# Decoding weights with the sign taken by GpSimd, an earlier Exp table load, and new instruction orders

## The chip, the cores and the metric

The kernel runs on one core of one Trainium2 chip. The metric is the time of one execution in microseconds (us), lower is better. The core's engines are called PE (TensorE), DVE (VectorE), ACT (ScalarE), POOL (GpSimd) and SP (SyncE, which here only issues DMAs). Each engine executes its own instructions strictly in order and waits on semaphores for what other engines produce. PEld is the weight-load side of PE.

## The reference, cut to what matters

```python
def _attn_ref(q, k, v, f):                      # B, H, S, D = 8, 8, 576, 64
    scores = np.matmul(q, k.transpose(0, 1, 3, 2)) / np.sqrt(D)
    cum = np.cumsum(np.log(np.clip(f, 0.0001, 1.0)), axis=-1)
    scores = scores + cum[:, :, :, None] - cum[:, :, None, :]   # causal, upper part -1e9
    attn = np.exp(scores - scores.max(-1)); attn /= attn.sum(-1) + 1e-9
    return np.matmul(attn, v)

def _moe_ref(x, w_tok1, w_tok2, w_ch1, w_ch2):  # x: (8, 576, 512) = attention, heads side by side
    h = np.maximum(x^T @ w_tok1, 0) @ w_tok2    # mixes tokens: 576 -> 256 -> 576
    u = x + h^T
    return u + np.maximum(u @ w_ch1, 0) @ w_ch2 # mixes channels: 512 -> 1536 -> 512
```

The four weight matrices of the mixers are float64 in memory. The chip has no float64 arithmetic, so the kernel turns each weight into float32 itself ("decodes" it) from its two 32-bit words, and keeps a rounded high part and a low part for the matmuls.

## The kernel before, in words

**Two stages.** The attention stage covers about the first 392 us. It runs over 32 head pairs (called n0 to n31 here): scores on PE (`score`, L747, with a decay term `fall`, L774, for the six head pairs listed in ND, n0 among them, or a mask, L753), a combined add and row minimum on DVE (`rmin`, L788), Exp with its row sum on ACT (`expo`, L792), transposes on PE (L862) and their copies by ACT and DVE (L872, L870), the product with v on PE (L891). After every second pair, a half of a batch goes through the token mixer (L1245). The second stage is the channel mixer (`chunk`, L1047 to L1049 and L1128 to L1130). It covers the rest; its first products are woven into the last few microseconds of the attention stage.

**Weight decoding** runs beside the attention stage: nine pieces of the token weights early (five of 128x256, four of 128x288), then 24 units of the channel weights of 128x512 each. `decode` (L553) makes one piece in six operations before it is split:

- s1, ACT (L572): the float64's high word, read as a float32, times 2^-112, into `g`. This sets the exponent's range and keeps the sign.
- s2, DVE (L576): shift `g` left by three bits. This aligns exponent and mantissa and pushes the sign out.
- s3, DVE (L580): the exponent bits of `g` into `e`.
- s4, DVE (L584): the low word times that power of two, into `e`.
- s5, POOL (L588): `g` plus `e`.
- s6, DVE (L592): the sign bit of the high word, joined to `g` with a bitwise or.

Then POOL makes the high part (L492) and the low part (L495), and for a channel unit four sums of blocks (L631) and their two parts. `d_g`, the tile with `g` and `e`, has two buffers.

**Order of work.** `ORDER` holds, for every engine, the numbers of its operations in the sequence in which it executes them. A planner (`Plan.run`) only assigns buffers to that sequence. A number n:k stands for k operations from n on. SP's loads are paced in addition: the total of what lies behind a load in flight is kept near 1.2 MB.

**Start.** `decay` (L508) loads f, takes its logarithm on ACT (L526; the small operation of L524 before it brings in the logarithm's table), sums it up on DVE (L528), scales it by -8 on ACT (L536, a Copy) and writes it to DRAM (`decd`, L538), from which later head pairs read it. The first Exp instruction (L792) brings in the Exp table. `fill` (L545) makes 36 small matmuls whose result nobody reads; each needs a free PSUM bank, and the scores of one head pair take all eight banks.

Of the kernel before, what the change touches and what calls it, by code (L numbers as in the profile page):

```python
# [67 lines left out]
    ),  # L68
    DVE=(
# [369 lines left out]
def build(nc, env, dims):  # L439
# [30 lines left out]
    def d_dve(n, fast=False):  # L470
        return 70 + (0.52 if fast else 1.042) * n
# [37 lines left out]
    def decay():  # L509
# [3 lines left out]
        def row(i):  # L513
            return at(w)[:, i, :]
# [38 lines left out]
    def decode(loads, w, hi, lo, tok):  # L553
# [20 lines left out]
        def s2():  # L574
            low, high, g, e = tl()
            nc.vector.tensor_scalar(g, g, 3, None, op0=ALU.logical_shift_left)  # L576
# [960 lines left out]
```

## Time and profile before

| what | us |
|---|---|
| median of 3 runs | 925.55 (924.63 to 926.01) |
| the profiled execution | 927.18 |
| its span, first to last instruction | 925.4 |
| PE busy | 905.5 (98%) |
| PEld busy | 781.3 (84%) |
| DVE busy | 710.2 (77%) |
| ACT busy | 520.6 (56%) |
| POOL busy | 237.2 (26%) |

Shares are of the whole span, which joins stages with different limits. PE's busy time counts a matmul from its start to a modelled end, so a short wait between two matmuls can vanish in it; the weight loads of PEld have no such tail. POOL has nothing to do after the attention stage.

### The profile page before, as it was taken

Reading aid. Unit: us, or ns where it says so; the run is one execution under the profiler, and the core shown is the slowest. Engines: PE = TensorE matmul, PEld = TensorE weight load, DVE = VectorE, ACT = ScalarE, POOL = GpSimd, SP = SyncE. Lnnn points to the kernel's source line nnn. Section 1 sums busy time; section 2 is a strip of 40 time slices with the busy share of each in tenths; the row PEclk is TensorE's granted clock in tenths of the full one; section 3 lists DMA queues with packets and bytes.
Section 4 is the critical chain, followed back from the end, with each engine's and each line's share of the span. In section 5 each row is a group of like instructions: output and inputs, shape, how many; then the busy total and the mean of one; then the engine's idle time right before and its main releaser. Section 6 shows DMA issues by size and latency. Waiting matters only on the chain.

```text
span 925.4 us, 26760 instructions
## 1 busy us (share of the span) xinstructions
PE 905.5 (98%) x10270; PEld 781.3 (84%) x10270; DVE 710.2 (77%) x1894; ACT 520.6 (56%) x1340; POOL 237.2 (26%) x320
## 2 busy tenths in 40 slices
PE   7999999999998999999999999999999999999998
PEld 5688888788887787888888888888888899999998
DVE  7998988888777777754699646986389955995497
ACT  5989998998788988731354123541135412542142
POOL 4577776766665562110000000000000000000000
PEclk9999999999999999999999999999999999999999
DMA  7999999998999698558887878888888799889986
GB/s 237 273 268 281 312 280 292 302 282 274 276 304 285 207 271 224 167 176 293 263 257 234 265 208 245 250 252 261 261 244 247 239 294 303 286 273 298 294 286 220
DMA packets 143871, 242.49 MB, mean 262 GB/s; under 512 B 15936, under 2 KB 71488, under 8 KB 143744
## 3 DMA queue, kind: packets, MB, share of 16 engines
q1 hardware_dynamic: 143648, 240.64, 84.8%
q8 instruction: 81, 1.33, 0.6%
q14 instruction: 46, 0.38, 0.1%
q10 hardware_dynamic: 96, 0.15, 0.0%
HBM read 199.52 MB, written 41.21 MB: 260 GB/s over the span
## 4 chain that ended last, share of the span: by engine, by line
PE 59%; DVE 2%; DMA 2%; POOL 1%; issue 0%; ACT 0%; SPq 0%; DVEq 0%; POOLq 0%
PE bank L1047 9%; PE bank L1049 9%; PE bank L1048 9%; PE bank L1128 9%; PE bank L1130 9%; PE bank L1129 9%; PE bank L1245 2%; DMA d_raw<-ud 1%; DVE pr L788 1%; PE bank L891 1%; PE bank L862 0%; DMA wq<-wd 0%; DMA recd<-rs 0%; POOL sg L495 0%; PE bank L747 0%
## 5 line engine op out<-in xcount | busy, mean ns | idle before, releaser
L792 ACT ACTIVATE pr<-pr,nmin 64x64 f32<-64x64 f32 (+4 forms) x320 | 176.7, 560 | 16.6 <-DVE nmin L788 16.2
L489 ACT ACTIVATE st<-H 128x512 fp32r<-128x512 f32 (+1 forms) x210 | 119.6, 586 | 89.0 <-PE bank L1129 63.3
L1128 PE MATMUL bank<-st,wq 128*128 128x512 f32 (+1 forms) x420 | 154.2, 367 | 0.3 <-DMA wq<-wd 0.3
L1130 PE MATMUL bank<-st,wq 128*128 128x512 f32 (+1 forms) x420 | 154.3, 367 | 0.0
L1129 PE MATMUL bank<-st,wq 128*128 128x512 f32 (+1 forms) x420 | 154.2, 367 | 0.0
L788 DVE CUSTOM_DVE_ANT_0 pr<-bank,cb 128x448 f32<-128x448 f32 (+3 forms) x260 | 108.7, 454 | 6.0 <-PE bank L747 1.8
L747 PE MATMUL bank<-raw 64*64 64x448 f32 (+6 forms) x1408 | 109.5, 397 | 2.6 <-DMA raw<-in_qk 1.3
L498 DVE TENSOR_TENSOR st<-H,st 128x512 fp32r<-128x512 f32 (+1 forms) x150 | 92.4, 631 | 14.6 <-ACT st L489 14.2
L891 PE MATMUL bank<-pf,vr 64*64 64x256 f32 (+3 forms) x2048 | 98.7, 317 | 1.5 <-ACT pf L872 0.5
L983 DVE TENSOR_TENSOR tmp<-bank,tmp 128x512 f32<-128x512 f32 (+1 forms) x80 | 50.2, 632 | 55.6 <-PE bank L1049 42.4
L872 ACT ACTIVATE pf<-bank 128x512 f32<-128x512 f32 x152 | 84.4, 596 | 11.2 <-PE bank L862 5.7
L1128 PEld LDWEIGHTS bank<-st,wq 128*128 128x128 f32 x420 | 78.8, 188 | 10.2 <-issue 0.6
L1130 PEld LDWEIGHTS bank<-st,wq 128*128 128x128 f32 x420 | 78.8, 188 | 9.9
L1129 PEld LDWEIGHTS bank<-st,wq 128*128 128x128 f32 x420 | 78.8, 188 | 9.6
L891 PEld LDWEIGHTS bank<-pf,vr 64*64 64x64 f32 x2048 | 76.4, 134 | 10.0 <-issue 2.0
L747 PEld LDWEIGHTS bank<-raw 64*64 64x64 f32 x1408 | 52.0, 132 | 27.7 <-issue 10.2
L1073 ACT ACTIVATE H<-bank 128x512 f32<-128x512 f32 (+1 forms) x30 | 16.5, 554 | 103.2 <-PE bank L1049 103.1
L1059 ACT ACTIVATE tmp<-bank 128x512 f32<-128x512 f32 (+1 forms) x30 | 16.6, 552 | 101.1 <-PE bank L1049 101.1
L862 PE MATMUL bank<-ident,pr 64*128 64x64 f32 x1536 | 65.0, 225 | 5.4 <-issue 2.1
L862 PEld LDWEIGHTS bank<-ident,pr 64*128 64x128 f32 x1536 | 58.8, 139 | 11.2 <-issue 5.0
L922 POOL TENSOR_TENSOR xt<-xt,rb 128x64 f32<-128x64 f32 (+1 forms) x64 | 52.5, 840 | 49.7 <-DVE xt L910 19.6
L792 ACT ACTIVATION_READ_ACCUMULATOR pr<-pr,nmin 128x1 f32 (+1 forms) x320 | 63.2, 198 | 0.0
(171 smaller groups left out, 2109.9 us busy)
## 6 DMA issues: line engine op xcount, KB each, us to landing
wq<-wd SPq DMA_DIRECT2D x420, 256.0 KB
raw<-in_qk SPq DMA_DIRECT2D x32, 576.0 KB
cb<-decd SPq DMA_DIRECT2D x26, 576.0 KB
d_raw<-in_w_ch SPq DMA_DIRECT2D x48, 256.0 KB
wd<-sg SPq DMA_DIRECT2D x24, 512.0 KB
vr<-in_v SPq DMA_DIRECT2D x64, 160.0 KB
rb<-recd SPq DMA_DIRECT2D x32, 320.0 KB
wd<-sg SPq DMA_DIRECT2D x24, 384.0 KB
```

What stands on the lines that cost most here:

```text
L489: nc.scalar.activation(out, in_, func, scale=scale)
L498: nc.vector.tensor_tensor(out, in_, asf(hi), op=ALU.subtract)
L747: nc.tensor.matmul(at(buf)[HALF[h], of : of + n], q[:, i0 : i0 + D], k[:, j0 : j0 + n], start=t not in (0, 1), stop=not nd, skip_group_che ...
L788: nc.vector.tensor_tensor_reduce(o, x, y, -1.0 / D**0.5, c0[:m, NS + z : NS + z + 1] if t == 5 else 3e38, op0=ALU.add, op1=ALU.min, accum_ ...
L792: nc.scalar.activation(x, x, AF.Exp, bias=E["nmin"][sm][:m, t : t + 1], scale=-1.0, accum_out=E["rec"][rm][:m, c : c + 1])
L862: nc.tensor.transpose(at(ps[s])[:, k * D : (k + 1) * D], at(pr)[r, x, :, :].rearrange("p a b -> p (a b)"), E["ident"][r, r])
L872: p.op("ACT", d_act(512), lambda src_=src_, o=o: nc.scalar.activation(o(), src_(), AF.Copy), rd=[ps[s]], wr=[(pt, s)], bufs=[ps[s], pt])
L891: nc.tensor.matmul(at(av[z])[o, 256 - w : 256], at(vr)[r, vblk(j), :], at(pt)[r, c : c + w], start=j == 4, stop=gi == 2, skip_group_check= ...
L1047: nc.tensor.matmul(o, wt[:, 0, :], h_, start=(first and k == 0), stop=False, skip_group_check=True)
L1128: nc.tensor.matmul(o, wt[:, 0, :], h_, start=(first and x == 0), stop=False, skip_group_check=True)
L1129: nc.tensor.matmul(o, wt[:, 1, :], h_, start=False, stop=False, skip_group_check=True)
L1130: nc.tensor.matmul(o, wt[:, 0, :], l_, start=False, stop=(x == FX - 1), skip_group_check=True)
```

## The change

The sign is no longer taken from the high word at the end. GpSimd multiplies the scaled `g` by 0.0, which leaves a zero that has the sign of `g`, in `e`. VectorE then shifts `g` and joins that sign in one instruction (the new s6, which stands where s2 stood). s3, s4 and s5 follow as before; what was the last operation of a decode is gone. Per decode DVE has three instructions instead of four and POOL two instead of one. DVE has 33 operations less in all, POOL 33 more.

In `decay`, an Exp of the one-column tile `lnx` stands just before the Copy of L536, so the Exp table is brought in there.

`ORDER` is new for all five engines in the attention stage. Most operations move by some places (PE by at most 15, SP and ACT by at most 22); the channel mixer's part is kept. The core of the diff, with the head of each order:

```diff
 PE:
-14:12 145 135 146 136 26:2 139 155 28:3 156 140 185 31:11 193 202 42:3 188 45:4 165 49 168 171 ...
+14 145 135 139 15:3 136 146 140 18 155:2 19:20 193 185 202 188 39:10 165 168 171 ...
 DVE:
-6 8:3 53:3 62 153 63 57 64 137:2 147 149 71 66 72 143 151 73 161 159 157 141 163 80:2 ...
+6 8:3 54:3 63 138 64 143 65 149 153 137 147 151 72 157 73:2 161 159 141 163 81:3 ...
 ACT:
-3:3 7 11 52 61 70 154 150 144 152 79 162 142 160 158 148 164 88 197 195 ...
+4 3 5 7 11 52 61 70 150 154 148 152 158 79 164 142 144 160 201 162 88 195 ...
 POOL:
-0 56 58:2 65 67:2 74 76 83 77 85:2 92 94 101 95 103:2 110 ...
+0 53 62 57:3 66 71 67:2 75 80 84 76 85 77 86 89 98 93:2 102 95 103:2 107 116 111 ...
 SP:
-2 1 132 51 50 60 181 69 12:2 133:2 78 184 87 182 ...
+2 1 132 51 50 60 69 133 181 12:2 182 134 78 184 87 ...
 decay:
+        def neg():
+            nc.scalar.activation(E["lnx"], E["lnx"], AF.Exp)
+            return nc.scalar.activation(row(0), row(1), AF.Copy, scale=-8.0)
-        p.op("ACT", d_act(S, False), lambda: nc.scalar.activation(row(0), row(1), AF.Copy, scale=-8.0), rd=["c"], wr=["f"], bufs=[w])
+        p.op("ACT", d_act(S, False), neg, rd=["c"], wr=["f"], bufs=[w])
 decode:
         def s2():
             low, high, g, e = tl()
-            nc.vector.tensor_scalar(g, g, 3, None, op0=ALU.logical_shift_left)
+            nc.gpsimd.tensor_scalar(asf(e), asf(g), 0.0, None, op0=ALU.mult)
+
+        def s6():
+            low, high, g, e = tl()
+            nc.vector.scalar_tensor_tensor(g, g, 3, e, op0=ALU.logical_shift_left, op1=ALU.bitwise_or)
-        def s6():
-            low, high, g, e = tl()
-            nc.vector.scalar_tensor_tensor(g, high, 0x80000000, g, op0=ALU.bitwise_and, op1=ALU.bitwise_or)
-        p.op("DVE", d_dve(w, True) , s2, wr=[gb], bufs=[gb], port=True)
+        p.op("POOL", d_pts(w), s2, port=True, rd=[gb], wr=[(gb, 1)], bufs=[gb])
+        p.op("DVE", d_dve(w), s6, port=True, rd=[(gb, 1)], wr=[gb], bufs=[gb])
         p.op("DVE", d_dve(w, True) , s3, rd=[gb], wr=[(gb, 1)], bufs=[gb], port=True)
         p.op("DVE", d_dve(w) , s4, port=True, rd=rd, wr=[(gb, 1)], bufs=[rb, gb])
         p.op("POOL", d_ptt(w), s5, port=True, rd=[(gb, 1)], wr=[gb], bufs=[gb])
-        p.op("DVE", d_dve(w), s6, port=True, rd=rd, wr=[gb], bufs=[rb, gb])
```

In these numbers 14 to 49 are the fills; 145, 135, 139 and 155 the four score groups of n0 and 146, 136, 140, 156 their decay terms; 185, 193, 202 and 188 the scores of n1; 165, 168, 171 the transposes of n0. On SP 132 and 181 load q and k of n0 and n1, 133 and 134 v of n0, 182 a half of v of n1, 50 to 78 token weights, 12 and 13 write `decd`, 184 reads it for n1. On DVE 137 to 163 (odd, and 138) are the row minima of n0; 53 to 55 and 57 belonged to the first decode before, 54 to 56 do now (54 is the join).

## Rows read from the trace of the kernel before

**Rows 1.** Windows: us; PE, PEld, DVE, ACT, POOL busy (instructions); clock; DMA; GB/s.
```profile
9.43:57.00 47.57, 43.22 (x834) 32.14 (x832) 47.19 (x187) 40.69 (x121) 28.51 (x40) 1.00 0.90 259
57.00:120.00 63.00, 62.66 (x1310) 52.83 (x1304) 56.58 (x214) 57.83 (x179) 47.43 (x63) 1.00 0.95 295
120.00:250.00 130.00, 127.87 (x2629) 108.51 (x2630) 111.18 (x399) 114.49 (x336) 90.42 (x116) 1.00 0.93 285
250.00:345.00 95.00, 90.80 (x1878) 77.87 (x1871) 73.18 (x276) 80.64 (x240) 57.07 (x77) 0.98 0.89 266
345.00:392.00 47.00, 45.01 (x934) 39.01 (x929) 36.35 (x122) 38.35 (x111) 7.48 (x9) 1.00 0.73 203
392.00:925.00 533.00, 529.66 (x2678) 467.16 (x2669) 381.42 (x686) 185.30 (x350) 3.43 (x4) 1.00 0.83 258
```

**Rows 2.** Windows of the start, same columns.
```profile
8.00:13.80 5.80, 5.23 (x70) 3.09 (x73) 4.30 (x16) 1.33 (x4) 2.54 (x4) 1.00 0.74 228
13.80:25.00 11.20, 9.34 (x158) 6.32 (x158) 11.08 (x52) 11.19 (x34) 5.94 (x10) 1.00 0.89 272
```

**Rows 3.** Windows, line L576 alone: DVE busy (instructions).
```profile
9.43:57.00 47.57, 3.47 (x11) 1.00 0.90 259
57.00:345.00 288.00, 11.50 (x22) 0.99 0.92 281
```

**Rows 4.** Groups by line and shape, DVE, 9 to 60 us: busy us, mean ns.
```profile
L592 DVE SCALAR_TENSOR_TENSOR d_g<-d_raw,d_g 128x256 uint32<-128x256 uint32 x5 | 2.1, 415 | 0.0
...
L592 DVE SCALAR_TENSOR_TENSOR d_g<-d_raw,d_g 128x288 uint32<-128x288 uint32 x4 | 1.8, 448 | 0.0
```

**Rows 5.** Groups by line and shape, POOL, whole span.
```profile
L492 POOL TENSOR_SCALAR sg<-d_g 128x512 fp32r<-128x512 f32 x48 | 30.5, 640 | 10.2 <-DVE d_g L592 7.6 <-DMA wd<-sg 1.7
...
L492 POOL TENSOR_SCALAR t1h<-d_g 128x256 fp32r<-128x256 f32 x5 | 2.2, 447 | 4.8 <-DVE d_g L592 4.8
L492 POOL TENSOR_SCALAR t2h<-d_g 128x288 fp32r<-128x288 f32 x4 | 2.0, 501 | 2.6 <-DVE d_g L592 2.6
```

**Rows 6.** Timeline of the start: start us, us, what [idle before, releaser].
```profile
2.96 0.20 ACT L524 ACTIVATE lnx<-rec 128x1 f32<-128x1 f32 x1
...
4.43 0.68 ACT L526 ACTIVATE xt<-xt 128x576 f32<-128x576 f32 x1 [1.27 <-DVE xt L525]
...
6.61 0.68 ACT L536 ACTIVATE xt<-xt 128x576 f32<-128x576 f32 x1 [1.49 <-DVE xt L528]
...
8.57 0.79 SPq L538 DMA_DIRECT2D decd<-xt  x2
...
9.43 0.29 DVE L576 TENSOR_SCALAR d_g<-d_g 128x256 uint32<-128x256 uint32 x1 [1.51 <-ACT d_g L572]
...
13.71 1.28 ACT L792 ACT_TABLE_LOAD   x1
...
15.00 0.35 ACT L792 ACTIVATE pr<-pr,nmin 64x64 f32<-64x64 f32 x1
```

**Rows 7.** Waits: us in total, times, longest; POOL in 9 to 57 us.
```profile
POOL d_g L588 <- DVE d_g L584: 13.2, 5, 6.8
```

**Rows 8.** Waits of the whole span.
```profile
DVE d_g L592 <- POOL d_g L588: 2.3, 3, 1.0
```

**Rows 9.** Timeline of PE at the start.
```profile
4.22 2.50 PE L545 MATMUL bank<-ident 128*64 128x48 f32 x22
...
8.00 1.85 PE L747 MATMUL bank<-raw 64*64 64x448 f32 x20 [1.28 <-DMA raw<-in_qk]
...
14.64 1.67 PE L545 MATMUL bank<-ident 128*64 128x48 f32 x22
```

**Rows 10.** Line L545: duration ns min/median/max, first and last start.
```profile
L545 PE MATMUL bank<-ident x72: 222/222/343, 1.8 to 22.2; 128*64 128x48 f32 x72
```

**Rows 11.** Timeline around 289 us.
```profile
289.29 0.89 PE L862 MATMUL bank<-ident,pr 64*128 64x64 f32 x19 [2.12 <-issue]
```

**Rows 12.** Window behind it, columns as in rows 1.
```profile
289.80:293.20 3.40, 3.40 (x66) 3.23 (x64) 1.50 (x3) 3.40 (x10) 3.40 (x4) 0.50 0.76 246
```

399 rows, old and new, of tables (ACT, DVE, PE, POOL) are left out of this document.

## The prediction

> **What bounds the kernel now.** I read the page's busy shares first, then windows cut where the limits change, then the groups by line, the waits, and the timeline of the first 25 us. The windows decide it [rows 1]. From 392 us on PE is busy 529.66 of 533.00 us; no instruction there is changed, so those 533 us stay. The attention stage has two parts. From 9.43 to 57 us DVE is busy 47.19 of 47.57 us, while PEld is busy 32.14 (68%). After 57 us PEld has 83 to 84% in every stretch, and PE is idle only 0.34 + 2.13 + 4.20 + 1.99 = 8.66 us up to 392 us. So DVE sets the pace up to 57 us: it leaves 0.38 us unused in 47 us, and PE, at 43.22 us busy, starves in between (its matmul tails hide part of that, the weight loads do not). From 57 us on PE is close to its own limit, with DVE at 241 of 288 us up to 345 us [rows 1]: DVE time saved there mostly becomes idle time.
>
> The front of the stage is therefore where the change can pay. Microseconds that DVE loses or gains before 57 us move all that comes behind, because behind it PE has a full queue.
>
> **The change part by part.** The sum is made against the profiled execution, 927.18 us (span 925.4, and 1.8 around it); the median of the runs is 925.55, 1.63 below it. I carry the difference over to the median.
>
> *Shift gone from DVE.* One DVE instruction per decode, s2, goes. In the DVE-bound stretch that is 11 instructions with 3.47 us [rows 3]. The new join takes the place of s6; both read two SBUF operands in one pass, so I take 415 ns at 128x256 and 448 ns at 128x288 for both [rows 4]: no difference. The trace shows no such join; below, it could cost no less than the shift alone, 3.47/11 = 0.315 us, which would add 11 x 0.1 = 1.1 us of gain, and I put the same 1.1 us above. Term: -3.47.
>
> *Sign on POOL.* 33 more POOL instructions, each like L492's one-input pass: 447, 501 and 640 ns [rows 5]. Between 9.43 and 57 us that is 5 x 0.447 + 4 x 0.501 + 2 x 0.64 = 5.5 us on an engine that is busy 28.51 of 47.57 us [rows 1], so it fits. But the first join now stands behind it: DVE's first decode instruction starts at 9.43 us right behind ACT [rows 6], and now starts one POOL pass later. That is 0.447 us and hand-overs, say 0.55; between 0.45 and 0.9 (the second sign stands directly behind the first). DVE has nothing else to do then, so this is lost. Later joins stand further behind their signs in the order. At the other end of a decode the way gets shorter: the hand-over from s5 to DVE and back to POOL is gone. Term: +0.55.
>
> *What queues behind a waiting join.* DVE executes in order, so behind a join that waits stand row minima, and behind those ACT's Exp and PE's transposes. POOL in turn often stands still on s5, waiting for s4: 13.2 us in 5 waits in the same stretch [rows 7], and a sign behind such an s5 waits with it. Before, DVE waited for POOL in s6, 2.3 us in 3 of 33 cases [rows 8]. I take nothing beyond that; the upper end is rival A.
>
> *Exp table.* ACT loads it from 13.71 for 1.28 us, right in front of the first Exp at 15.00 [rows 6]. The new Exp stands behind L526, which ends at 4.43 + 0.68 = 5.11; the Copy behind it waits 1.49 us for DVE's scan, until 6.61. Load and one-column instruction take 1.28 + 0.20 = 1.48 us and fill that gap to 0.02 us, so the Copy and the two writes of `decd` at 8.57 do not move. If the cover were gone it would cost 1.28 us on that branch, which has 8.57 - 7.29 = 1.28 us of slack. What is gained: between 13.80 and 25 us ACT is busy 11.19 and DVE 11.08 of 11.20 us [rows 2], both full. Taking 1.28 us from ACT alone leaves DVE as the limit, so it adds nothing to DVE's term but lets it come through. Between 0 and -1.28, I take 0.
>
> Of the same step the Trainium skill ("ScalarE: Activation LUTs", section What ACT_TABLE_LOAD costs) says that a switch costs a load of about 1283 ns and a drain of about 1380 ns. The row agrees with the load (1.28) and not with the drain: the first Exp starts 0.01 us behind the load. With the drain the Copy would come about 1.4 us later and the `decd` writes at most 0.2 us later, so the sum would stay.
>
> *Fills and first scores.* Before, 12 fills stood ahead of the first scores, and PE worked through most of them from 4.22 to 6.72 us. The new order keeps one; PE then waits for q and k until 8.00 us [rows 9]. The first 22 fill matmuls take 2.50/22 = 0.114 us each, 22 later ones 1.67/22 = 0.076, and single ones last 343 ns at most against 222 in the median [rows 9, 10]. So PE ran at the lower of its two clock levels at first and had reached the higher one when scores began. The window's clock column shows 1.00 there, which the pace contradicts. Now the first scores begin after about 4 us of idling, likely at the lower level. At half the clock the 5.23 us of work in 8.00 to 13.80 us [rows 2] lasts up to 5.2 us longer. DVE has the joins, s3 and s4 of two decodes to do meanwhile, some 2.5 us at 0.42 each. Between 0 and 5.2 I take 1.0, nearer the low end, since the new order then runs all scores and 20 fills without a gap. Term: +1.0.
>
> The Trainium skill ("TensorE: Matmul & The Clock Gate", section What's actually happening) has the same behaviour as a rule: the array starts throttled and sustained activity releases it. The trace agrees by the fills' pace, 0.114 against 0.076 us.
>
> *57 to 345 us.* DVE loses 22 shifts, 11.50 us [rows 3], POOL gains 22 x 0.64 = 14.1 us on 195 of 288 us [rows 1, 5]. PE is idle 0.34 + 2.13 + 4.20 = 6.67 us there. From -6.7 (all of it) to +2 (POOL's queue delays the products that release the token mixer); I take about an eighth of PE's idle time: -0.9.
>
> *New orders elsewhere.* q and k of n1 are issued behind two other loads (a 262 kB weight piece and a v half); the PE operation that needs them stands behind 20 fills now. Taken as 0, between -1 and +1.
>
> Sum: -3.47 + 0.55 + 1.0 - 0.9 = -2.8 us. The profiled execution would be 924.4, the median 922.7.
>
> **The rivals.**
>
> *A: joins wait for POOL and the gain is eaten.* For: POOL's 13.2 us of standing on s5 [rows 7], in order, with signs behind; against: POOL has 19 us free before 57 us. At 0.25 us per join, 11 joins take 2.8 us: 925.5.
>
> *B: slower, PE starts at the low clock and stays there.* Place: PE, 8 to about 20 us. If low until the first transposes at 20 us, the 5.2 us above come in full and some 2 us more from the scores of n1 and the fills in front of them (a fifth of the 9.34 us of PE work in 13.80 to 25 us [rows 2], where PE has free time to make up the rest). I count 7 us against gains of 3.8 without the 1.0: +3.2, 928.7. It decides from 3.8 + 1.85 = 5.65 us of delay on. For: 11 fills are moved from idle time to behind scores; each needs a bank that DVE has to free. Against: scores, decay terms and fills stand close together there.
>
> *C: more comes through.* PE stood still for 2.12 us with nothing that the profile shows, and the granted clock was then 0.50 for 3.40 us [rows 11, 12]. That is 2.12 + 1.70 = 3.8 us that need not recur with another order. With it: 918.9. The same time results if half of PE's idle time after 57 us goes. Against: such a pause may come at another place.
>
> *D: it does not do what it says.* The early Exp brings no table, or the first real Exp loads it again. That leaves 1.28 us on ACT at 13.7 us: 924.
>
> **How the numbers follow.** Forecast 0.40 (920.5 to 924), A with D 0.25, B 0.20, C 0.15. What a measurement here can tell from no change is about 0.2%, 1.85 us: faster is below 923.7. Faster: C and nine tenths of the forecast and a little of D, 0.53. Within: the rest of the forecast, most of A, 0.25. Slower: B and some of A's worse end, 0.22. The range from 917.5 to 928.5 takes in C with its 1.1 us for a cheaper join, and B almost to its price.
>
> **What would show it.** Right: DVE's first decode instruction starts near 10.0 us; a table load at 5.1 us and none at 13.7; the scores of n4 and what follows begin 2 to 4 us earlier than before, at an unchanged distance from there to the end; three DVE instructions per decode. Wrong: idle time of DVE ahead of the joins with POOL as releaser, over 3 us before 57 us (A); the granted clock or the score matmuls at half pace beyond 13 us (B); the lead at 57 us lost or doubled by 392 us.

## The result

The changed kernel takes 932.62 us (median of 4 runs, 931.96 to 934.91) against 925.09 us before: a ratio of 1.0085 (95% interval 1.0065 to 1.0104), 7.5 us slower. The forecast was 922.7 us, and faster.

The page of the changed kernel opens with the engines' busy time:

```profile
PE 906.9 (97%) x10270; PEld 781.3 (84%) x10270; DVE 705.8 (76%) x1861; ACT 521.6 (56%) x1341; POOL 279.0 (30%) x353
```

DVE has 33 instructions less, POOL 33 more, as meant. But POOL's busy time grew from 237.2 to 279.0 us, by 41.8 us: 1.27 us for each new instruction, where the forecast had 0.45 to 0.64. The groups of POOL by line and shape name it (L579 is the new sign):

```profile
L579 POOL TENSOR_SCALAR d_g<-d_g 128x512 f32<-128x512 f32 x24 | 36.0, 1501 | 14.2 <-ACT d_g L575 14.2
L491 POOL TENSOR_SCALAR sg<-d_g 128x512 fp32r<-128x512 f32 x48 | 31.2, 651 | 1.4 <-DMA wd<-sg 1.0
...
L579 POOL TENSOR_SCALAR d_g<-d_g 128x256 f32<-128x256 f32 x5 | 4.2, 849 | 5.8 <-ACT d_g L575 5.8
...
L579 POOL TENSOR_SCALAR d_g<-d_g 128x288 f32<-128x288 f32 x4 | 3.7, 930 | 1.1 <-ACT d_g L575 1.1
```

The sign takes 849, 930 and 1501 ns; L491 (the former L492 of [rows 5]) still takes 651 ns for the same 512 columns. The waits of the whole span show who pays (us in total, times, longest):

```profile
DVE d_g L583 <- POOL d_g L579: 18.1, 15, 3.6
```

L583 is the new join. DVE stands still for POOL 18.1 us, where it did so for 2.3 us before [rows 8], and behind the join stand the row minima that ACT and PE need. The windows, with the stretches and columns of [rows 1]:

```profile
9.43:57.00 47.57, 42.21 (x818) 32.54 (x812) 44.53 (x173) 38.63 (x120) 37.61 (x51) 1.00 0.83 251
57.00:120.00 63.00, 60.57 (x1280) 50.75 (x1281) 55.32 (x196) 54.37 (x160) 53.90 (x64) 1.00 0.92 283
120.00:250.00 130.00, 126.56 (x2556) 106.66 (x2549) 105.58 (x383) 113.13 (x342) 103.08 (x127) 1.00 0.92 278
```

Up to 57 us DVE is no longer full (44.53 of 47.57 us against 47.19). Between 57 and 250 us PE is idle for 5.9 us where it was idle for 2.5, and gets 3836 matmuls done instead of 3939. The lateness shows in one row per kernel, that of the weight loads of the scores, whose last number is the start of the last one. First the kernel before, then the changed one:

```profile
L747 PEld LDWEIGHTS bank<-raw x1408: 129/133/135, 8.0 to 372.6; 64*64 64x64 f32 x176
```

```profile
L750 PEld LDWEIGHTS bank<-raw x1408: 128/133/228, 7.4 to 378.6; 64*64 64x64 f32 x176
```

The last score starts 6.0 us later; from there to the end it is 552.5 us (931.1 - 378.6) against 552.8 (925.4 - 372.6). So the loss arose in the attention stage, and the channel mixer neither adds nor gives back anything.

The start of ACT in the changed kernel (timeline, as [rows 6]) shows the early Exp where it should be:

```profile
4.73 0.68 ACT L529 ACTIVATE xt<-xt 128x576 f32<-128x576 f32 x1 [1.59 <-DVE xt L528]
5.43 1.28 ACT L519 ACT_TABLE_LOAD   x1
6.73 0.20 ACT L519 ACTIVATE lnx<-lnx 128x1 f32<-128x1 f32 x1
6.91 0.68 ACT L520 ACTIVATE xt<-xt 128x576 f32<-128x576 f32 x1
...
14.95 0.67 ACT L795 ACTIVATE pr<-pr,nmin 128x448 f32<-128x448 f32 x1 [0.85 <-DVE nmin L791]
```

The load is hidden, no second one stands ahead of the first real Exp, and yet that Exp starts at 14.95 us (15.00 before): it waits for a row minimum. PE's start (timeline, as [rows 9]) shows why, in part:

```profile
7.39 3.90 PE L750 MATMUL bank<-raw 64*64 64x448 f32 x28 [3.12 <-DMA raw<-in_qk]
```

28 score matmuls take 3.90 us, 0.139 each, where 20 took 1.85, 0.093 each [rows 9]: PE starts at a lower pace, as one of the steps had it, though the granted clock of the window from 8.00 to 13.80 us reads 1.00 in both profiles. (Widths are mixed in both rows; a run below has the same 28.)

### The profile page after: what moved, and what is told of

The parts are those of the page before. It is cut to its first block, busy times and chain, and to the rows that moved or that the text cites. A ratio compares the mean times of both kernels' runs of the same rounds, so it can differ in the third digit from the quotient of the medians.

```text
span 931.1 us, 26767 instructions
## 1 busy us (share of the span) xinstructions
PE 906.9 (97%) x10270; PEld 781.3 (84%) x10270; DVE 705.8 (76%) x1861; ACT 521.6 (56%) x1341; POOL 279.0 (30%) x353
## 4 chain that ended last, share of the span: by engine, by line
PE 76%; DMA 8%; DVE 6%; POOL 5%; ACT 2%; issue 2%; SPq 1%; DVEq 0%; ACTq 0%; POOLq 0%
PE bank L1050 9%; PE bank L1051 9%; PE bank L1052 9%; PE bank L1131 9%; PE bank L1132 9%; PE bank L1133 9%; PE bank L1248 7%; PE bank L750 5%; PE bank L894 4%; PE bank L865 3%; DVE pr L791 2%; DMA cb<-decd 2%; POOL d_g L579 1%; DMA raw<-in_qk 1%; DMA wd<-sg 1%
## 5 line engine op out<-in xcount | busy, mean ns | idle before, releaser
L795 ACT ACTIVATE pr<-pr,nmin 128x320 f32<-128x320 f32 (+4 forms) x320 | 176.8, 557 | 14.1 <-DVE nmin L791 13.3
L750 PE MATMUL bank<-raw 64*64 64x448 f32 (+6 forms) x1408 | 114.0, 403 | 6.5 <-DMA raw<-in_qk 3.1
L894 PE MATMUL bank<-pf,vr 64*64 64x128 f32 (+3 forms) x2048 | 97.9, 315 | 0.7 <-ACT pf L875 0.3
L750 PEld LDWEIGHTS bank<-raw 64*64 64x64 f32 x1408 | 55.3, 134 | 35.4 <-issue 11.5
L865 PEld LDWEIGHTS bank<-ident,pr 64*128 64x128 f32 x1536 | 59.4, 139 | 11.1 <-ACT pr L795 2.6
L494 POOL TENSOR_TENSOR sg<-d_g,sg 128x512 fp32r<-128x512 f32 x48 | 62.1, 1298 | 1.0
```

The source lines that it names most:

```text
L750: nc.tensor.matmul(at(buf)[HALF[h], of : of + n], q[:, i0 : i0 + D], k[:, j0 : j0 + n], start=t not in (0, 1), stop=not nd, skip_group_che ...
L795: nc.scalar.activation(x, x, AF.Exp, bias=E["nmin"][sm][:m, t : t + 1], scale=-1.0, accum_out=E["rec"][rm][:m, c : c + 1])
L865: nc.tensor.transpose(at(ps[s])[:, k * D : (k + 1) * D], at(pr)[r, x, :, :].rearrange("p a b -> p (a b)"), E["ident"][r, r])
L894: nc.tensor.matmul(at(av[z])[o, 256 - w : 256], at(vr)[r, vblk(j), :], at(pt)[r, c : c + w], start=j == 4, stop=gi == 2, skip_group_check= ...
```

## The experiments

Times are medians; each ratio is against the kernel before in runs on the same chip. That kernel's median was 925.04 us beside the first four runs, 925.42 beside the next four and 926.26 beside the last three, so small differences between runs of different groups are read from ratios.

**The sign as a two-step instruction.**

```diff
-nc.gpsimd.tensor_scalar(asf(e), asf(g), 0.0, None, op0=ALU.mult)
+nc.gpsimd.tensor_scalar(asf(e), asf(g), 0.0, -0.0, op0=ALU.mult, op1=ALU.add)
```

> The changed kernel with the sign made by a two-step instruction on GpSimd (times 0.0, plus -0.0, which keeps the sign) in place of the one-step multiply. Theory S (the price of the sign): the one-step form costs 1.50 us at 128x512 where the two-step L492 costs 0.64; POOL becomes late and the joins wait. Then the sign falls to about 0.64 us, POOL's busy time from 279 to 255 us, the joins' waits from 18 us to under 8, and the time from 932.6 to 926 to 928 us. Theory O (the new orders are worse by themselves): the sign gets cheaper but the time stays over 930.5. Theory C (cold start alone): the 2.1 us that n2 is late stay, and with them nearly all of the loss; over 930.5.

Measured: 922.11 us, ratio 0.9967 (0.9950 to 0.9983). A second step in this one instruction is worth 10.5 us. POOL's busy time is 253.1 us, 25.9 less. The sign's group in POOL, and the join's wait:

```profile
L579 POOL TENSOR_SCALAR d_g<-d_g 128x512 f32<-128x512 f32 x24 | 15.3, 639 | 18.6 <-ACT d_g L575 18.6
```

```profile
DVE d_g L583 <- POOL d_g L579: 7.0, 6, 2.3
```

The join waits 11.1 us less. The last score starts at 368.2 us, 10.4 us earlier than in the changed kernel:

```profile
L750 PEld LDWEIGHTS bank<-raw x1408: 129/133/227, 7.3 to 368.2; 64*64 64x64 f32 x176
```

Theory S holds, and by more than it said: the whole loss was the price of the sign, and with the price that the forecast had used the kernel is faster than before. Theories O and C fall as causes of the loss.

**Which two-step form.**

```diff
-nc.gpsimd.tensor_scalar(asf(e), asf(g), 0.0, None, op0=ALU.mult)
+nc.gpsimd.tensor_scalar(asf(e), asf(g), 0.0, 1.0, op0=ALU.mult, op1=ALU.mult)
```

> The changed kernel with the sign as a two-step instruction of two multiplies (times 0.0, times 1.0). Theory F1 (a form with its second step left out is the slow one, any two-step form is quick): the sign costs about 0.64 us at 128x512 and the time is 921 to 924, as with times and plus. Theory F2 (only the pair times and plus is quick): the sign costs 1.5 us or more and the time is 931 to 934.

Measured: 922.07 us, ratio 0.9969 (0.9944 to 0.9994). The sign takes as long as with the plus:

```profile
L579 POOL TENSOR_SCALAR d_g<-d_g 128x512 f32<-128x512 f32 x24 | 15.3, 638 | 16.4 <-ACT d_g L575 16.4
```

F1 holds: what is slow is the form with its second step left out.

**Is it POOL's time or the join's wait?** The quick sign, and behind it a one-step multiply into a tile that nobody reads:

```diff
+nc.gpsimd.tensor_scalar(asf(e), asf(g), 0.0, -0.0, op0=ALU.mult, op1=ALU.add)
+n = {256: 87, 288: 92, 512: 252}[w]
+return nc.gpsimd.tensor_scalar(E["waste"][:, :n], E["mask"][:, :n], 0.0, None, op0=ALU.mult)
```

> The quick sign with, behind each one, an extra one-step multiply on GpSimd into a tile that nobody reads, 87, 92 or 252 columns wide, so that POOL is busy as long as with the slow sign (about 0.42, 0.43 and 0.84 us more) but the join need not wait for it. Theory W (the join's wait is what costs, since row minima stand behind it on DVE): most of the gain stays, 922 to 926. Theory P (POOL's occupancy costs, because later signs, sums and the scaling of the attention output come late): 929 to 934.

Measured: 924.6 us, ratio 0.9980 (0.9959 to 1.0001). The idle instruction and the join's wait:

```profile
L581 POOL TENSOR_SCALAR waste<-mask 128x252 f32<-128x252 f32 x24 | 20.3, 845 | 0.0
```

```profile
DVE d_g L585 <- POOL d_g L579: 8.0, 7, 2.5
```

POOL is about as busy as with the slow sign (25.4 us in the idle instructions), but the join waits 8.0 us and not 18.1, and the kernel is 1.2 us (by the ratios) to 2.5 us (by the medians) slower than with the quick sign alone; the intervals overlap, and their width leaves room for up to about 4 us. So theory W holds: the same microseconds on POOL cost about 10 us in front of the join and, by the middle values, a tenth to a quarter of that behind it. The idle instruction reads other data and has the one-step price too: 252 columns take 845 ns, 256 columns of the sign 849.

**Where the loss arises.** The slow sign for the nine token pieces alone:

```diff
+if hi:                                                       # a token piece
     nc.gpsimd.tensor_scalar(asf(e), asf(g), 0.0, None, op0=ALU.mult)
+else:
+    nc.gpsimd.tensor_scalar(asf(e), asf(g), 0.0, -0.0, op0=ALU.mult, op1=ALU.add)
```

> The one-step sign for the nine token pieces, the two-step sign for the 24 channel units. The changed kernel is 2.9 us behind the quick sign when n5 starts and 10 us at the end. If each part's loss stays as it arose: 922.1 plus 2 to 3, 924 to 926 (24 units make the other 7 us). If the start's loss is made good later: 922. If the start decides all: over 930.

Measured: 924.04 us, ratio 0.9977 (0.9956 to 0.9997): 0.9 us by the ratios and 1.9 by the medians over the quick sign, with overlapping intervals. The start's share is small; the rest, some 8 to 10 us by difference, comes with the 24 channel units, most of which are decoded after 57 us. Its profiled execution is longer than its median (span 927.5), so its times are not read. The other profiles agree: when the scores of n5 start, the changed kernel is 3.0 us behind the quick sign with the plus and 1.8 us behind that with two multiplies (60.0 against 57.0 and 58.2 us), and 10.4 us behind both at the last score.

**The fills.** The first 12 fills back ahead of the first scores, with the slow sign and with the quick one:

```diff
-14 145 135 139 15:3 136 146 140 18 155:2 19:20 193 ...
+14:12 145 135 139 136 146 140 155:2 26:13 193 ...
```

> The changed kernel with the first 12 fills put back ahead of the first scores, nothing else. Theory C: the first scores run at the higher clock level again, their 28 matmuls at 8 us take 2.1 instead of 3.9 us, n2 starts about 2 us earlier and the whole time falls by about 2 us, to 930.6. Theory S: the first scores get quicker, but DVE waits for the signs there anyhow; under 1 us, 931.6 to 932.6.

> The quick sign (times 0.0, plus -0.0) and the first 12 fills ahead of the first scores. With the slow sign the fills changed nothing (933.3 against 932.6). Theory C (the cold start is paid for once DVE no longer waits for signs): n2 starts 1 us or more earlier than the 25.0 us of the quick sign alone, and the time is 921 or less. Theory S (the early lead is lost again within the next head pairs): 921.5 to 923.5.

Measured: 933.32 us with the slow sign, ratio 1.0087 (1.0067 to 1.0107), against 932.62; 921.62 us with the quick one, ratio 0.9956 (0.9938 to 0.9974), against 922.11. PE's timelines, first with the slow sign, then with the quick one (L559 are the fills, L761 the scores):

```profile
4.20 1.96 PE L559 MATMUL bank<-ident 128*64 128x48 f32 x22
7.45 2.07 PE L761 MATMUL bank<-raw 64*64 64x448 f32 x28 [1.30 <-DMA raw<-in_qk]
```

```profile
4.22 2.58 PE L559 MATMUL bank<-ident 128*64 128x48 f32 x22
7.83 3.61 PE L761 MATMUL bank<-raw 64*64 64x448 f32 x28 [1.02 <-DMA raw<-in_qk]
```

In the profile with the slow sign the fills do what theory C says: the 28 matmuls take 2.07 us in place of 3.90. In the one with the quick sign they do not: 3.61 us, against 3.51 with the quick sign and no fills in front. And with the slow sign the lead does not last: the scores of n2 start 1.25 us earlier than in the changed kernel (24.80 against 26.05 us), those of n3 at the same time (36.00 against 36.01). In between, the granted clock was 0.50 in this profile (1.00 in that of the changed kernel):

```profile
23.00:26.00 3.00, 3.00 (x40) 2.18 (x40) 2.96 (x12) 3.00 (x9) 1.38 (x3) 0.50 0.76 271
26.00:29.00 3.00, 3.00 (x31) 1.35 (x28) 1.97 (x8) 2.92 (x11) 2.32 (x4) 0.50 0.67 180
```

So the fills in front change neither time beyond the intervals, but no profile with the new orders has a quick start that was kept, and what the slow start costs by itself stays open. With the quick sign DVE is busy 21.99 of 22.20 us from 13.80 to 36 us, whether the fills stand in front or not, so a lead of PE could hardly come through there. With the slow sign neither expected time was met; with the quick sign it is theory S's. 921.62 us is the fastest median of all, but not clear of the quick sign alone.

**The early Exp alone,** in the kernel before, and the quick sign without it:

```diff
+nc.scalar.activation(E["lnx"], E["lnx"], AF.Exp)             # added to the kernel before
```

```diff
-nc.scalar.activation(E["lnx"], E["lnx"], AF.Exp)             # taken from the quick sign's kernel
```

> The kernel before with the early Exp alone (old decode, old orders). Theory S: this part costs nothing; the load stands from 5.1 to 6.4 us, none at 13.7, and the time is 925.1 or up to 1.3 us below. Theory T (the early load itself is late work: it holds up the Copy and the writes of the decay terms): 926 to 928.

> The quick sign without the early Exp: the table is loaded in front of the first Exp again. Theory Z (another engine is late there, the load is hidden): 922.1, within 0.7. Theory T (the load of 1.28 us lies on the path once the decode is quick): 923 to 924.

Measured: 925.3 us, ratio 1.0003 (0.9984 to 1.0021), and 922.28 us, ratio 0.9967 (0.9944 to 0.9990). ACT in the kernel before with the early Exp:

```profile
5.15 1.28 ACT L520 ACT_TABLE_LOAD   x1
6.45 0.20 ACT L520 ACTIVATE lnx<-lnx 128x1 f32<-128x1 f32 x1
6.63 0.68 ACT L521 ACTIVATE xt<-xt 128x576 f32<-128x576 f32 x1
...
12.96 0.33 ACT L796 ACTIVATE pr<-pr,nmin 64x64 f32<-64x64 f32 x1
```

In the kernel before, the first Exp starts 2.0 us earlier (its first scores, too, start 0.5 us earlier, at 7.49 us), and the last score starts at 373.7 us against 372.6: no gain reaches the end. Both middle values lie with theories S and Z; the intervals are some 2 us to either side, so the 1 us that theory T meant is not excluded.

**Decode and orders apart.** The new decode in the old orders, with the slow and with the quick sign; and the new orders with the old decode. The numbers of the operations are mapped onto the other order:

```diff
# new decode in the old orders, DVE and POOL per decode
-DVE  ... s2 ... s3 ... s4 ... s6 ...      POOL ... s5 ...
+DVE  ... join ... s3 ... s4 ...           POOL ... sign ... s5 ...
# old decode in the new orders
-DVE  ... join ... s3 ... s4 ...           POOL ... sign ... s5 ...
+DVE  ... s2 ... s3 ... s4 ... s6 ...      POOL ... s5 ...
```

> New decode (one-step sign) and early Exp in the old orders: the join stands where the shift stood, the old join is gone, each sign stands in POOL's order at the first operation that began after its input was ready. Theory S: the sign's 1.5 us hit these orders too, less well placed: 930 to 936. Theory O: with the old orders the loss goes: 922 to 926.

> The quick sign and the early Exp in the old orders, signs placed as in the run with the slow sign (952.4). Theory S: the sign's price made most of that loss; 925 to 932. Theory O (where the sign stands in POOL's and DVE's order decides): over 935, since an early sign that waits for ACT holds up all of POOL behind it.

> The new orders and the early Exp with the old decode: no sign on GpSimd, the shift where the join stands, the old join placed behind the sum of its decode. Theory D (the gain of the quick sign over the kernel before, 3 us, is DVE's saved shift): the gain is gone, 925 to 930. Theory O (it is the new orders): 920.5 to 923.5.

Measured: 952.39 us, ratio 1.0298 (1.0272 to 1.0325) with the slow sign in the old orders; 935.4 us, ratio 1.0109 (1.0061 to 1.0157) with the quick one; 933.82 us, ratio 1.0093 (1.0056 to 1.0131) for the new orders with the old decode. The slow sign costs 17 us in the old orders, more than in the new ones. And neither the quick decode nor the new orders gain time as a whole without the other; each alone loses 8 to 10 us. The slow sign in the old orders (theory S: 930 to 936) and the new orders alone (theory D: 925 to 930) both came out above what was expected. The 935.4 us do not tell theory S from theory O (925 to 932, over 935). The places of the signs in the old orders and of s6 in the new ones are mine, so these runs bound the parts only roughly.

Where each loses and gains shows in the times at which the scores of a head pair start (its first weight load, us; at each of these points PE has done the same number of matmuls, within two, in all five kernels):

| kernel | n10 | n24 | n29 | n31 | last score |
|---|---|---|---|---|---|
| before | 110.6 | 280.2 | 342.9 | 367.2 | 372.6 |
| changed | 115.5 | 290.8 | 350.8 | 373.0 | 378.6 |
| changed, quick sign | 110.5 | 280.5 | 340.4 | 362.5 | 368.2 |
| new orders, old decode | 119.3 | 291.3 | 352.5 | 374.6 | 380.4 |
| old orders, quick decode | 115.7 | 291.0 | 351.6 | 376.3 | 381.7 |

The new orders with the old decode lose their 8 to 9 us up to n10. From n29 to n31 they gain: all nine profiles with the new orders take 22.2 us there, whatever the decode, and all four with the old orders 24.0 to 24.8 us, for the same 466 matmuls.

## Why the prediction was wrong

**The step that failed** is "33 more POOL instructions, each like L492's one-input pass: 447, 501 and 640 ns". L492 is a two-step instruction, the sign as written has one step, and the trace before held no one-step `tensor_scalar` of GpSimd at all. I took the nearest row for the thing itself and put no bound above it, although this was the one new operation of the change. It measured 849, 930 and 1501 ns; a two-step sign measures 404, 461 and 639. Put that price in, and the kernel takes 922.11 us; the forecast was 922.7.

**From the price to the time.** Against the quick sign POOL is busy 25.9 us longer, 24.8 of them in the 33 signs; the join's waits went up by 11.1 us (18.1 against 7.0), the kernel by 10.5. The waits up to 57 us and from 57 to 392 us, first in the changed kernel, then with the quick sign:

```profile
DVE d_g L583 <- POOL d_g L579: 2.5, 3, 1.8
DVE d_g L583 <- POOL d_g L579: 15.6, 12, 3.6
```

```profile
DVE d_g L583 <- POOL d_g L579: 1.8, 2, 1.2
DVE d_g L583 <- POOL d_g L579: 5.2, 4, 2.3
```

Rival A had the right mechanism, in-order DVE behind a join that waits, but a price of 0.25 us per join in the first 57 us alone, and its sign there (over 3 us of such waits) did not show: 2.5 us. Of the 11.1 us, 10.4 arise after 57 us, where I had counted DVE time as nearly free: I had weighed the work there (11.5 us of shifts gone) and not a wait in DVE's queue, which stops the row minima as well. In the trace of the changed kernel 14 joins wait longer than 0.3 us; a row minimum is among the next six instructions of DVE behind 13 of them, and PE stands still for 6.0 us in all from the start of these waits to 4 us behind the joins. With the quick sign six joins wait that long, and PE does not stand still there. Not tested is whether a part of the loss comes from the decode being ready later, and not from what stands behind the join: no run moved the joins back in DVE's order so that they need not wait.

**First join, one POOL pass later (+0.55 us).** It starts at 10.01 us, as the forecast said, but by luck: ACT had its input ready 0.3 us earlier than before (the sign starts at 9.12 us, the shift had started at 9.43), and the slower sign used that up (9.12 + 0.85 = 9.97 us). With the quick sign it starts at 9.39:

```profile
9.39 0.43 DVE L583 SCALAR_TENSOR_TENSOR d_g<-d_g 128x256 uint32<-128x256 uint32 x1 [1.23 <-POOL d_g L579]
```

**Shift gone (-3.47 us before 57 us).** The right sum at the wrong place: that the forecast of 922.7 us lies so near the quick sign's 922.11 is in good part luck. With the quick sign DVE is busy 45.90 of 47.57 us in that stretch, so it did get free, but the way to the end got shorter only later. And over the whole span DVE's busy time fell by 8.1 us (710.2 to 702.1) and not by the 15.0 us of the shifts: at 128x512 the join averages 789 ns where the old s6 averaged 728, for which I had taken no difference, and s4 758 ns where it averaged 689. The windows of that kernel:

```profile
9.43:57.00 47.57, 42.61 (x864) 33.88 (x859) 45.90 (x177) 40.45 (x124) 33.36 (x51) 1.00 0.88 263
57.00:120.00 63.00, 62.29 (x1312) 53.15 (x1306) 56.18 (x208) 57.09 (x174) 51.83 (x67) 1.00 0.99 289
120.00:250.00 130.00, 125.73 (x2612) 107.40 (x2612) 105.43 (x383) 114.09 (x338) 94.97 (x129) 1.00 0.94 285
250.00:345.00 95.00, 93.67 (x1962) 80.06 (x1956) 74.10 (x287) 83.12 (x248) 59.03 (x81) 1.00 0.93 281
345.00:392.00 47.00, 46.55 (x912) 40.01 (x903) 36.58 (x114) 37.23 (x107) 10.58 (x13) 1.00 0.69 184
```

Up to 250 us PE does 4788 matmuls, 15 more than before [rows 1], so it has no lead worth a microsecond there; from 250 to 345 us it does 1962 against 1878. That the new orders with the old decode are 8.4 us slower than before, and the quick decode in the old orders 10.0, says that the 3 us are made by the two together. By the table above the lead arises behind n24: it is 4.4 us at the last score in these two profiles.

**New orders elsewhere (0, between -1 and +1).** Mis-sized: 2.0 us of that lead arise from n29 to n31, and the new orders gain them with every decode (PE is busy 46.55 of 47.00 us from 345 to 392 us, where it was busy 45.01 [rows 1]). Another 2.9 us arise from n24 to n29, where the profile before has its pause of 2.12 us and the lower clock behind it [rows 11, 12], the gain of rival C. But the quick sign's profile has a pause as well, at another place, as rival C's counter-argument had it, with the granted clock at 1.00 from 175.6 to 179.0 us behind it:

```profile
175.62 0.38 PE L750 MATMUL bank<-raw 64*64 64x192 f32 x4 [2.77 <-issue]
```

So the pauses are no clear part of the 3 us between the medians. Of the 59 executions of the kernel before that ran beside the experiments, the 13 with a mean granted clock of 1.00 have a median of 925.1 us and the other 46 one of 925.9. And the changed kernel, with 1.00 in all four executions and no such pause in its profile, is slower all the same.

**A misreading.** From 250 to 345 us PEld is busy 82% (77.87 of 95.00 us [rows 1]) and not 83 to 84; no term hangs on it.

**Early Exp (0).** Right, as far as the runs can tell: the load is hidden and gains no time. The drain of which the Trainium skill tells ("ScalarE: Activation LUTs", section What ACT_TABLE_LOAD costs) is not in the trace: the load ends at 5.43 + 1.28 = 6.71 us and the next instruction starts at 6.73. Rival D falls: there is no second load.

**Fills and first scores (+1.0).** The slow start is there, 0.139 against 0.074 us per matmul (3.90/28, and 2.07/28 in the profile with the fills in front), and its price is not measured: putting the fills back changed the time by +0.7 and -0.5 us, inside the intervals, but no profile with the new orders kept a quick start. Rival B falls on two other rows: in the changed kernel the next 16 score matmuls, from 13.62 us, take 1.09 us, 0.068 each, so the low pace did not last; and the quick sign, with 3.51 us for the same first 28, is faster than the kernel before. B was the rival with the sign of the result and not its cause.

**57 to 345 us (-0.9).** For POOL's occupancy alone I allowed up to +2; idle instructions that make POOL as busy as the slow signs, over the whole stage, cost 1.2 to 2.5. What was missing is the wait in front of the join.

## What to carry to other kernels

Price a new instruction from a row of the same form on the same engine; when the trace has none, the range must hold a multiple of the nearest row, and one run with a form that is known to be quick settles it. When work is moved from one in-order engine to another and its result comes straight back, the new instruction's time can be paid, as here, by everything that stands behind the instruction that waits for it, far more than by the engine that executes it. Orders and work belong together: here each without the other, fitted in by hand, was slower than neither.

## What the runs showed of the hardware

On GpSimd a one-step `tensor_scalar` (a multiply, no second operation) on float32 took 849 ns for 256 columns and 1501 for 512: 2.55 ns per column. With a second step, a plus or a multiply, it took 404 and 639 ns: 0.92 ns per column. With one step more it is quicker by a factor of 2.3 at 512 columns; the idle instruction, on other data, had the one-step price as well. Why is open.

The join, L583, which reads two SBUF operands, averaged 914 ns at 128x512 with slow signs beside it, 850 with quick signs and idle instructions, and 789 with quick signs alone; POOL's busy time was 279.0, 276.7 and 253.1 us. At 128x256 it was the other way round (423 ns with slow signs, 492 with quick ones), so what makes it longer is not settled.

The same 12 fills ahead of the first scores had two outcomes: with 1.96 us for 22 fill matmuls the next 28 score matmuls took 2.07 us, with 2.58 us they took 3.61. PE stood still for 2 to 3 us, with nothing that the profile shows as the cause, in the kernel before (2.12 us, up to 289.29 us; the granted clock was then 0.50 [rows 12]) and with the quick sign (2.77 us, up to 175.62 us; the granted clock was then 1.00).
